# Modulation columns by one-column products, their later sums by 32 by 32 transposes, and a new order table

## The chip, the cores and the metric

The kernel runs on one core of a Trainium2 chip. The metric is the device time of one execution in microseconds (us). Five engines work side by side, each through its own list of instructions in a fixed order: TensorE (PE, with its weight loads as PEld), VectorE (DVE), ScalarE (ACT), GpSimd (POOL) and SyncE (SP), which issues nearly all of the DMAs. An instruction waits until its operands are there, and everything behind it on its engine waits with it.

## The reference, cut to what matters

One transformer block over 2048 rows of 576 numbers: a modulation vector from `c`, a linear attention with 32 heads of 18, and a feed-forward block with 4608 hidden units.

```python
mod = (_silu(c) @ w_mod).reshape(c.shape[0], 6, 1, -1)   # 576 -> 6 x 576
sa, ca, ga, sb, cb, gb = (mod[:, i] for i in range(6))
h = _layernorm(x) * (1 + ca) + sa
x = x + ga * _A_ref(h, A_wqkv, A_wo)      # linear attention: phi(q), phi(k), k^T v, divided by q . sum(k)
h = _layernorm(x) * (1 + cb) + sb
x = x + gb * _B_ref(h, B_w1, B_w2)        # silu(h @ w1) @ w2
```

The change touches how `mod` is summed. Its first third (`sa`, `ca`) is needed before any product with `h` can begin; the other two thirds (`ga`, `sb` and `cb`, `gb`) are needed much later.

## The kernel before, in words

Rows lie in 16 tiles of 128 (`x`, `acc`), the 576 columns in four chunks of 128 and a tail of 64. Numbers are split in a high and a low part, so that a product is three products of narrower numbers: for each chunk, high by high, low by high and high by low. Every operand therefore needs a high part (a cast, mostly by ACT, `w_hi`, `split_h`) and a low part (full minus high, by DVE or POOL, `w_lo`, `sub_hi`).

**The start.** `load_x`, `load_mod0` and `load_w` (lines 425 to 465) fetch row tiles, the first third of `w_mod` in four chunks of 128 rows (`mods`, in tiles called hT) with the last 64 rows apart (`tmod`), and the weights of K and Q (in tiles called acc). `load_mod0` fetches first the columns 0 to 256 of both halves, then the columns 256 to 576. Then:

- DVE multiplies each chunk of `w_mod` rows by silu(c), one number per partition (`sc`), and adds them up (`add_rows`, lines 517 and 519): four instructions for the first 256 columns and four for the other 320.
- TensorE sums over the 128 partitions. For the first two column chunks this is a product whose stationary operand is the summed tile and whose moving operand is a column of ones (`mod_cols`, line 528). For the rest the summed rows are the moving operand and the result is one row (`mod_rows`, line 539), which ACT and DVE copy out (`copy_row`, lines 543 and 544) and TensorE turns into columns (`turn_rows`, line 550).
- DVE adds 1 to the scale column (`add_cols`, line 533), applies shift and scale to the transposed rows (`modulate`, lines 360 and 362), and `split_h` makes high (line 366) and low part (line 262) of the result. `k_part` (line 574) multiplies them by the K weights for tiles 0 and 1. `keep_busy` (line 568) fills gaps on TensorE with products of ones that nobody reads.

**Stage A.** From there on K and Q of all tiles are projected (line 929), phi is applied (lines 936 to 942 and 495), k^T x is accumulated over blocks of four tiles (`sum_steps`: products in line 1054 in two PSUM rooms, psG0 and psG1, added to SBUF by DVE in line 1064), and the rows of the next block are normalised, turned and split (`block_steps`, `turn_steps`: lines 354, 1021, 362 and 998).

**The two later thirds of the modulation** (`mod_steps`) run beside stage A: SP loads chunks of `w_mod` into four rooms, ACT scales them (line 1102), POOL adds them up (line 1104, eight adds for each third), SP stores the sum of 128 partitions (590 KB) to DRAM (line 1105), ACT's queue loads it back so that the 128 partial sums of 9 columns lie side by side in a partition (line 1108), DVE sums them (line 1111), and SP stores the vector (line 1112).

**Attention's output and the MLP.** From 200 us to 360 us the output of attention, the second layer norm and the first group of hidden units run, in PSUM rooms called `big` (three of two banks) and `small` (two of one bank); `down_add` (line 1449) empties a `big`. From 360 us on come the other 17 groups, in PSUM rooms called `up` (line 1925) and `down` (line 2009) that take over the same eight banks.

**What sets the order.** The program is first written out by its loops and a planner; then `arrange(ORDERS, begun)` (called in line 2380, written in line 252) makes each engine follow a table of numbers, `ORDERS`: which of the instructions written out comes first, second and so on. The table covers everything up to some 460 us (2,991 of TensorE's products and 656 of DVE's instructions). Behind it the planner's own order stands. On SP the table also sets the order of the DMAs.

Of the kernel before, what the change touches and what calls it, by code (L numbers as in the profile page):

```python
# [24 lines left out]
def kernel(ctx: ExitStack, tc, A_x, A_wqkv, A_wo, B_x, B_w1, B_w2, c, w_mod, out):  # L25
# [33 lines left out]
    def behind(instructions):  # L59

        with ExitStack() as order:
# [7 lines left out]
            0-43 45-46 52 49-50 44 47-48 53-54 51 65 57-58 61-62 66-72 55-56 59-60 63-64 73-77 82-83 80-81 78-79  # L69
            116 84-87 90-91 124 88-89 92-105 117 106-111 125 118-123 112-115 126-141 154-173 142-147 174-177  # L70
            148-153 210-217 178-179 246-249 180-181 250-251 290-291 182-201 218-221 256-267 274-289 202-209
            292-295 302-319 222-227 320-329 228-237 268-273 330-331 296-299 332-335 300-301 336-337 238-245
            252-255 342-343 338-341 344-353 366-367 354-365 368-391 412-413 398-403 392-395 414-423 396-397
            406-411 424-425 436-439 426-427 440-445 404-405 446-451 428-435 452-457 462-463 458-461 464-517
            524-527 518-519 530-533 520-523 534-553 572-573 586-587 574-575 554-571 588-591 598-601 528-529
            592-595 602-609 596-597 610-629 576-579 630-645 580-585 646-653 658-661 682-685 662-669 686-687
            692-697 688-689 698-701 654-657 670-673 690-691 702-703 674-681 704-763 770-771 764-769 772-787
            826-829 788-825 838-843 862-865 830-833 844-845 866-867 846-857 872-875 834-837 890-891 876-877
            892-893 878-889 894-901 858-861 868-871 926-931 902-925 932-943 950-951 944-945 952-963 946-949
            978-983 1000-1001 966-977 984-999 1002-1015 1022-1027 1016-1021 1028-1029 964-965 1030-1075  # L80
            1084-1085 1076-1077 1102-1117 1086-1093 1130-1135 1118-1119 1078-1079 1120-1121 1136-1137 1122-1129
            1138-1139 1080-1083 1140-1145 1094-1095 1160-1161 1096-1101 1146-1157 1172-1177 1162-1171 1158-1159
            1248-1249 1178-1183 1250-1253 1184-1185 1254-1257 1186-1199 1208-1213 1258-1259 1285-1286 1200-1207
            1287-1292 1214-1219 1236-1237 1220-1227 1238-1247 1228-1235 1293-1300 1260-1284 1301-1339 1352-1356
            1340-1351 1357-1386 1413-1417 1387-1412 1418-1439 1446-1450 1440-1445 1451-1488 1507-1510 1489-1494
            1511-1513 1495-1506 1514-1558 1573-1576 1601-1604 1559-1572 1605 1577-1586 1634 1638 1587-1600
            1606-1623 1646-1649 1624-1625 1650 1655-1660 1626-1633 1661-1670 1639 1635-1637 1640-1641 1687-1688
            1671-1678 1715-1719 1679-1680 1642-1643 1681-1682 1651 1689-1694 1652-1653 1644-1645 1695-1698 1654
            1699-1710 1720-1727 1711-1712 1728-1731 1713-1714 1683 1748 1684-1685 1732-1745 1749 1686 1746-1747
            1776-1779 1781-1784 1780 1762 1785-1790 1763-1765 1791-1792 1750 1793-1798 1751-1761 1766-1771  # L90
            1799-1802 1772-1775 1854 1803-1809 1821-1825 1870 1810 1855-1857 1811 1826-1827 1812-1813 1871-1873
            1828-1831 1874-1876 1832-1835 1877 1836-1839 1814-1816 1858-1860 1883-1886 1817-1819 1861-1862 1820
            1840-1843 1863-1864 1844-1853 1865-1868 1915-1918 1869 1878-1882 1887-1904 1976 1990 1977-1980
            1919-1921 1905-1906 1922-1926 1991 1981 1907-1908 1931-1934 1982 1909-1914 1983-1984 1927-1930 1985
            1935 1992 1936-1941 1986 1942-1947 1987-1989 1948-1967 1993-1995 1968-1972 2004-2010 1973-1975
            2011-2022 1996-1999 2023-2028 2000 2029-2036 2001-2003 2037-2038 2049-2069 2039-2048 2070-2081 2086
            2082 2098-2099 2087-2088 2106-2110 2089-2095 2100-2101 2083-2085 2096-2097 2115-2136 2102 2137-2142
            2147 2159-2160 2103-2105 2111-2113 2161-2162 2148 2114 2187-2190 2163-2166 2149 2143-2146 2167-2168
            2150 2169-2186 2151 2191 2199 2192-2194 2200-2202 2152-2153 2203-2210 2195 2213 2211-2212 2154-2158
            2196-2198 2214-2224 2231-2234 2225-2230 2239 2249 2259-2261 2240 2235-2238 2262 2245 2241-2242  # L100
            2246-2247 2243 2255-2258 2248 2244 2265-2270 2295 2263 2250-2254 2271 2264 2272-2274 2296-2298
            2283-2284 2299-2305 2285-2287 2309 2288-2291 2277-2278 2292-2293 2310-2311 2275-2276 2312-2313 2294
            2306-2308 2279-2282 2314-2323 2329-2333 2335 2324 2336-2339 2334 2347-2352 2340 2353-2354 2325-2328
            2355-2358 2341 2359-2363 2342 2364-2365 2343-2344 2366-2369 2345-2346 2370-2375 2377 2376 2378-2382
            2391-2398 2383-2387 2399 2388-2389 2400-2402 2390 2403-2407 2427-2428 2408-2412 2421 2433 2413-2420
            2422 2445-2446 2434 2423-2426 2429-2432 2447-2450 2463-2470 2439 2435-2438 2440-2444 2483-2489
            2451-2452 2490 2457-2458 2503 2459-2460 2504 2461 2453 2462 2454-2456 2555-2560 2477-2480 2505-2508
            2521-2528 2471-2475 2481 2476 2482 2541-2544 2567-2569 2491-2493 2570-2572 2497-2502 2494-2496
            2545-2548 2515-2518 2509-2514 2519-2520 2579-2584 2529-2539 2585 2540 2593-2595 2549-2554 2561-2562
            2596 2563-2564 2597-2600 2586 2565-2566 2607-2610 2573-2574 2611-2612 2575-2577 2587-2589 2578  # L110
            2590-2592 2619-2623 2601 2624-2626 2633-2640 2613-2618 2647-2651 2602 2652 2603-2606 2641-2646
            2659-2663 2627-2630 2665-2667 2631-2632 2664 2668-2678 2653-2658 2693-2696 2685-2692 2739-2741
            2679-2683 2742-2743 2699-2704 2684 2711 2744 2697-2698 2712-2718 2705-2710 2725-2732 2719-2724
            2757-2761 2733-2738 2745-2756 2762 2775-2781 2795 2873-2874 2796-2798 2875-2876 2782 2877-2878
            2783-2786 2763-2774 2799-2800 2787-2794 2801-2804 2815-2820 2805-2814 2833-2840 2853-2855 2891 2856
            2892 2821 2841-2843 2822 2844 2823-2832 2857-2860 2845-2852 2861 2893 2929-2933 2879 2862 2880 2934
            2909-2911 2863-2864 2881-2890 2894-2895 2865-2866 2896 2867-2871 2897 2935 2898-2905 2872 2912-2916
# [483 lines left out]
    for k in range(HEAD):  # L601
        mod_cols(k, tmod, sel, first=k == 0)
    turn_tiles(pT, (0, 1), START)
    for k in (1, 2, 3):
        add_rows(k, 0, c1)
# [1806 lines left out]
```

## Time and profile before

| | us |
|---|---|
| median of three runs | 1092.07 |
| lowest and highest | 1091.23, 1094.24 |
| the profiled execution | 1092.31 |
| its span, first to last instruction | 1090.6 |

Times in the profile are counted from the first instruction. In a row of the timeline stand the start, the time that the instruction or the merged run of instructions (x4: four of them) took, the engine, the line of the kernel, the operation, and what is written and read. In brackets stands how long the engine had been idle, and what ended that. A row of stretches gives the busy time of each engine in a stretch of the span, the granted TensorE clock (PEclk, 1.00 is full) and what the DMA engines moved.

### The profile page before, as it was taken

What the parts mean: (1) busy time and instruction counts of PE and PEld (TensorE: products, weight loads), DVE (VectorE), ACT (ScalarE), POOL (GpSimd) and SP (SyncE); (2) the same over time, 40 slices, a digit from 0 to 9 for tenths busy, and PEclk for the clock granted to TensorE, in tenths of its full rate; (3) what the DMA queues carried; (4) which work ended last, traced back from release to release, by engine and by line L of the source; (5) the groups of instructions that cost most, each with busy time, mean ns of one, the idle gap of its engine ahead of it and who ended that gap; (6) DMA issues with size and microseconds to landing.
All of it is one profiled execution on the core that took longest, in us unless ns stands there. A gap on an engine that the chain in (4) does not pass through costs nothing.

```text
span 1090.6 us, 19057 instructions
## 1 busy us (share of the span) xinstructions
PE 1064.8 (98%) x7027; PEld 758.6 (70%) x7027; DVE 913.4 (84%) x1438; ACT 708.5 (65%) x1318; POOL 741.3 (68%) x804
## 2 busy tenths in 40 slices
PE   8899999999999899999999999999999999999998
PEld 6899999899785455666666666666666666666665
DVE  7968968778889799998997888987987887898767
ACT  5766554246757686677667767776776776676554
POOL 3556615655725499879878778877788678677563
PEclk9999999999999999999999999999999999999999
DMA  9497665223256768478577667567657747616522
GB/s 292 123 214 174 64 182 130 54 81 106 66 183 224 206 239 249 136 229 247 176 204 244 172 194 224 197 207 221 201 168 254 206 137 264 208 63 201 169 79 109
DMA packets 119342, 193.51 MB, mean 177 GB/s; under 512 B 42892, under 2 KB 77584, under 8 KB 119248
## 3 DMA queue, kind: packets, MB, share of 16 engines
q1 hardware_dynamic: 86276, 190.81, 56.2%
q10 hardware_dynamic: 32972, 1.48, 3.1%
q8 instruction: 55, 0.90, 0.3%
q14 instruction: 39, 0.32, 0.1%
HBM read 176.77 MB, written 15.48 MB: 176 GB/s over the span
## 4 chain that ended last, share of the span: by engine, by line
PE 77%; DVE 12%; ACT 3%; DMA 3%; issue 3%; POOL 2%; SPq 0%; DVEq 0%; POOLq 0%; ACTq 0%
PE up L1925 30%; PE down L2009 29%; PE big L390 6%; PE psK L929 4%; PE psG L1054 3%; DVE hT L262 1%; PE small L1433 1%; PE big L1444 1%; PE psK L1224 1%; DVE acc L1021 1%; DMA hT<-in_B_w_dram 1%; DMA turned<-acc 1%; PE big L1358 1%; DVE w L262 1%; DMA hT<-in_w_mod_dram 1%
## 5 line engine op out<-in xcount | busy, mean ns | idle before, releaser
L1925 PE MATMUL up<-hT,w 128*128 128x512 f16 x1264 | 317.6, 379 | 2.6 <-ACT p L1900 1.6
L1925 PEld LDWEIGHTS <-w 128*128 128x128 f16 x1492 | 146.0, 98 | 140.0 <-issue 3.9
L2018 DVE SCALAR_TENSOR_TENSOR acc<-acc,set,down 128x576 f32<-128x576 f32 x128 | 103.4, 810 | 31.4 <-PE down L2009 30.5
L1943 ACT ACTIVATE f<-f,set 128x512 f32<-128x512 f32 x102 | 73.0, 718 | 59.7 <-DVE f L1949 50.4
L1963 POOL TENSOR_TENSOR s<-f,f 128x256 f32<-128x256 f32 x66 | 55.2, 836 | 73.2 <-ACT f L1944 70.8
L2009 PE MATMUL down<-w,hc 128*128 128x288 f16 x600 | 90.8, 286 | 0.4 <-ACT f L1939 0.4
L2009 PE MATMUL down<-w,hb 128*128 128x288 f16 x600 | 90.5, 286 | 0.2 <-DVE acc L2018 0.2
L2009 PE MATMUL down<-w,hT 128*128 128x288 f16 x480 | 82.9, 286 | 0.4 <-DVE acc L2022 0.4
L1947 DVE TENSOR_TENSOR f<-up,p 128x512 f32<-128x512 f32 x102 | 69.6, 682 | 15.1 <-PE up L1925 8.6
L1944 ACT ACTIVATE f<-f,set 128x512 f32<-128x512 f32 x102 | 73.6, 722 | 3.2
L2009 PEld LDWEIGHTS <-hb 128*128 128x128 f16 x600 | 58.7, 98 | 22.6 <-issue 0.7
L2009 PEld LDWEIGHTS <-hc 128*128 128x128 f16 x600 | 58.6, 98 | 22.5 <-DVE acc L2018 0.7
L1949 DVE TENSOR_TENSOR f<-up,f 128x512 f32<-128x512 f32 x68 | 46.9, 689 | 26.6 <-PE up L1925 25.5
L1987 POOL TENSOR_TENSOR hc<-s,hc 128x512 f16<-128x512 f32 x50 | 63.7, 1274 | 6.4 <-ACT hc L1983 6.4
L1967 POOL TENSOR_TENSOR f<-f,s 128x256 f32<-128x256 f32 x66 | 53.6, 812 | 18.5 <-DVE hb L1987 10.2
L1960 POOL TENSOR_TENSOR s<-f 128x256 f32<-128x256 f32 x66 | 55.9, 847 | 14.1 <-ACT f L1940 11.3
L2009 PEld LDWEIGHTS <-hT 128*128 128x128 f16 x480 | 46.9, 98 | 26.6 <-issue 0.8
L390 PE MATMUL big<-w,qT 128*128 128x288 f32 x352 | 59.6, 307 | 0.6 <-DVE acc L1372 0.6
L1965 POOL TENSOR_TENSOR s<-s,f 128x256 f32<-128x256 f32 x66 | 56.4, 854 | 3.6
L2009 PE MATMUL down<-w,ha 128*128 128x288 f16 x396 | 55.6, 286 | 0.3 <-DVE w L262 0.3
L2009 PE MATMUL down<-w,hd 128*128 128x288 f16 x396 | 55.5, 286 | 0.2 <-ACT hd L1983 0.2
L1987 POOL TENSOR_TENSOR hd<-s,hd 128x256 f16<-128x256 f32 x66 | 50.5, 765 | 6.6 <-ACT hd L1983 6.6
(408 smaller groups left out, 2830.1 us busy)
## 6 DMA issues: line engine op xcount, KB each, us to landing
hT<-hd SPq DMA_DIRECT2D x101, 640.0 KB, 5.2
hT<-hd SPq DMA_DIRECT2D x65, 512.0 KB, 3.9
hT<-in_B_w_dram SPq DMA_DIRECT2D x14, 576.0 KB, 5.1
hT<-in_B_w_dram SPq DMA_DIRECT2D x28, 256.0 KB, 6.4
raw<-in_B_w_dram SPq DMA_DIRECT2D x11, 576.0 KB, 4.4
v<-in_B_w_dram SPq DMA_DIRECT2D x9, 576.0 KB, 5.1
acc<-in_A_x_dram SPq DMA_DIRECT2D x16, 288.0 KB, 5.0
raw<-in_B_w_dram SPq DMA_DIRECT2D x9, 512.0 KB, 5.6
```

Source lines behind the costliest of these rows:

```text
L390: T.matmul(ps, xpart(a), wpart(b), start=n == 0, stop=n == len(XW) - 1)
L1925: T.matmul(ps, left, right, start=first and m == 0, stop=m == len(seq) - 1, skip_group_check=True)
L1943: A.activation(f, f, AF.Silu, scale=factor(self.g, "inv"))
L1944: A.activation(f, f, AF.Identity, scale=factor(self.g, "delta"))
L1947: V.tensor_add(f, self.bank[bank[1]], self.p1)
L1960: G.tensor_sub(self.s3, half(i, 0, 0), half(i, 0, 1))
L1963: G.tensor_add(self.s[:, 0:1], half(i, 0, 1), half(i, 1, 1))
L1965: G.tensor_sub(self.s[:, 1:2], self.s[:, 0:1], half(i, 0, 0))
L1967: G.tensor_sub(half(i, 1, 0), half(i, 1, 0), self.s[:, 1:2])
L1987: eng.tensor_sub(t[:, :, 1, :], src, t[:, :, 0, :])
L2009: T.matmul(ps[:, p, :HALF], left[:, u, p * P : (p + 1) * P], right[:, v], start=n in (1, 5, 7, 6) and j == 0, stop=j == len(passes) - 1, s ...
L2018: V.scalar_tensor_tensor(dst, dst, factor(self.g, "ratio"), ps[:, :, :HALF], op0=ALU.mult, op1=ALU.add)
```

## The change

Three things change.

1. `add_rows`, `mod_rows`, `copy_row` and `turn_rows` go. For each chunk of 128 rows of `w_mod` and each 128 of its columns TensorE now makes a product with that 128 by 128 block as the stationary operand and silu(c) as a moving operand of one column (`mod_part`), all added up in PSUM: 16 products for the first two column chunks, 24 for the other three. POOL copies the 64 tail columns beside themselves (`twice`), since the tail's columns are wanted in both halves of the partitions. Fourteen of the 33 `keep_busy` products go.
2. `mod_steps` no longer stores and loads the 590 KB. DVE transposes the sum in blocks of 32 by 32 (two instructions), sums each row of a block (a sum over 32 numbers), SP stores the 18 KB that are left and loads them with the four partition groups side by side, DVE sums those four, and SP stores the vector as before, in another order of elements.
3. Every number of `ORDERS` is new; the comment on the change says that the table comes from a model in which VectorE and GpSimd exclude each other. In the code that is written out, the last part of the K weights is loaded ahead of row tiles 2 and 3. The work outside 1 and 2 is the same, instruction for instruction.

```diff
     ORDERS = {
         "PE": """
-            0-43 45-46 52 49-50 44 47-48 53-54 51 65 57-58 61-62 66-72 55-56 59-60 63-64 73-77 82-83 80-81 78-79
+            0-29 38-42 45-49 30-33 50 34-37 43-44 51-56 65-70 79-90 57 59-60 63-64 73-74 139 58 61-62 71-72
...
-    colps = kvp[0][:, 1, 128:], kvp[2][:, 1, :]
+    colps = psT(), kvp[0][:, 1, 128:]
     colp = {k: colps[k >= HEAD][:, 2 * k : 2 * k + 2] for k in START}
...
+    def twice(m):
+        G.tensor_copy(m[..., D:DX], m[..., KC * P : D])
+
+    def mod_tail(js):
+        for j in js:
+            T.matmul(colp[j], tmod[:, j * P : (j + 1) * P], sel, start=j == js[0], stop=False, skip_group_check=True)
+
+    def mod_part(k, js):
+        for j in js:
             for a in range(2):
-                T.matmul(colp[k][:, a : a + 1], m[:, a, k * P : (k + 1) * P], rhs,
-                         start=first and a == 0, stop=last, skip_group_check=True)
+                T.matmul(colp[j][:, a : a + 1], mods[k][:, a, j * P : (j + 1) * P], sc[:, k : k + 1],
+                         start=False, stop=k == KC - 1, skip_group_check=True)
...
     w_hi(wk_, 1, acc[1])
-    for a in range(2):
-        mod_rows(a, 0)
-    first_k(1)
+    w_lo(wk_, 1, acc[1], V)
+    twice(tmod)
+    mod_tail(range(HEAD, KC + 1))
+    for k in range(KC):
+        twice(mods[k])
+        mod_part(k, range(HEAD, KC + 1))
+        if k < HEAD:
+            first_k(k)
+    add_cols(HEAD, KC + 1)
...
-        do("SP", 0.45, lambda: nc.sync.dma_start(parts, tmod2[:, :, 0:D]), ["tmod0", "tmod1"], [f"parts{piece}"], 8.0)
...
-        do("SP", 0.45, lambda: nc.scalar.dma_start(r, parts.rearrange("p a d -> p (a d)").rearrange("p (q j) -> q p j", j=NC9)),
-           [f"parts{piece}"], raws2[i], 14.0)
-        s9 = s9s[piece - 1]
-        do("DVE", 2.27, lambda: V.tensor_reduce(s9, r.rearrange("q p j -> q j p"), axis=AX.X, op=ALU.add), raws2[i], [f"s9{piece}"])
...
+        def turn():
+            for a in range(2):
+                V.transpose(r[:, a].rearrange("p (b i) -> p b i", i=32), tmod2[:, a, 0:D].rearrange("p (b i) -> p b i", i=32))
+
+        def fold():
+            V.tensor_reduce(some, flat.rearrange("p (b i) -> p b i", i=32), axis=AX.X, op=ALU.add)
+            nc.sync.dma_start(quarters, some)
+            nc.sync.dma_start(four, quarters.rearrange("(q c) b -> c q b", q=4))
+            V.tensor_reduce(total, four.rearrange("c q b -> c b q"), axis=AX.X, op=ALU.add)
```

Three places of the order are shown, each as it stood and as it stands. The first is the list of SP at the very start: xt are row tiles, hT the first third of `w_mod` (256 columns of both halves, then 320), acc0, acc1 and acc2 the weights of K and Q (the first five pieces are K's), acc3 with 128x4x576 the four row tiles of the next block. Before:

```order
L427 DMA xt_118<-in_A_x_dram 128x576 x2
L451 DMA hT_125<-in_w_mod_dram 128x2x256 x4
L394 DMA acc0_91<-in_A_wqkv_dram 128x576 x2
L451 DMA hT_125<-in_w_mod_dram 128x2x320 x4
L394 DMA acc0_91<-in_A_wqkv_dram 128x576 x2
L427 DMA xt_118<-in_A_x_dram 128x576 x2
L394 DMA acc1_92<-in_A_wqkv_dram 128x576
L396 DMA acc1_92<-in_A_wqkv_dram 64x576
L1005 DMA acc3_94<-in_A_x_dram 128x4x576
L397 DMA acc1_92<-in_A_wqkv_dram 64x576
```

And now:

```order
L426 DMA xt_118<-in_A_x_dram 128x576 x2
L450 DMA hT_125<-in_w_mod_dram 128x2x256 x2
L426 DMA xt_118<-in_A_x_dram 128x576
L450 DMA hT_125<-in_w_mod_dram 128x2x256
L426 DMA xt_118<-in_A_x_dram 128x576
L450 DMA hT_125<-in_w_mod_dram 128x2x256
L450 DMA hT_125<-in_w_mod_dram 128x2x320 x4
L393 DMA acc0_91<-in_A_wqkv_dram 128x576 x2
L959 DMA acc3_94<-in_A_x_dram 128x4x576
L393 DMA acc0_91<-in_A_wqkv_dram 128x576 x2
L395 DMA acc1_92<-in_A_wqkv_dram 64x576
L396 DMA acc1_92<-in_A_wqkv_dram 64x576
```

The first K weights moved from behind the first 256 modulation columns to behind all row tiles and all modulation columns, and the third K weight to behind the next block's rows as well.

The second place is DVE in stage A, from the first of block 1's sums to the third (sum0, sum1, sum2, read from psG0 and psG1). Before:

```order
L1064 TENSOR_TENSOR sum0_107<-psG1_117,sum0_107 128x576
L1064 TENSOR_TENSOR sum1_108<-psG0_116,sum1_108 128x576
L942 TENSOR_SCALAR acc1_92<-psK_220 128x576
L495 SCALAR_TENSOR_TENSOR acc1_92<-e_98,acc1_92 128x576
L362 TENSOR_SCALAR acc2_93<-acc2_93,col_a_84 128x512 x2
L1064 TENSOR_TENSOR sum2_109<-psG1_117,sum2_109 128x576
```

And now:

```order
L1018 TENSOR_TENSOR sum0_107<-psG1_117,sum0_107 128x576
L1018 TENSOR_TENSOR sum1_108<-psG0_116,sum1_108 128x576
L896 TENSOR_SCALAR acc1_92<-psK_233 128x576
L1067 STREAM_TRANSPOSE raw1_122<-tmod_381 128x576 x2
L1070 TENSOR_REDUCE crow_96<-raw1_122 128x36
L1018 TENSOR_TENSOR sum2_109<-psG1_117,sum2_109 128x576
```

The two transposes and the first sum of the last third of the modulation (tmod is what POOL's adds made) now stand ahead of sum2; the second step of phi and the two modulations of turned rows moved behind it.

The third place is DVE around the end of the first group of hidden units, where the PSUM rooms `big` give way to `up`. In the built program the first room `up` lies in the bank of big_3881 before, and in the bank of big_3935 now. Before:

```order
L1449 SCALAR_TENSOR_TENSOR acc3_94<-acc3_94,set0_99,big_3923 128x576
L268 SCALAR_TENSOR_TENSOR w_3657<-raw_3660,set0_99,w_3657 128x256
L1449 SCALAR_TENSOR_TENSOR acc3_94<-acc3_94,set0_99,big_3881 128x576
L268 SCALAR_TENSOR_TENSOR w_3657<-v_3658,set0_99,w_3657 128x256 x2
L268 SCALAR_TENSOR_TENSOR w_3657<-raw_3660,set0_99,w_3657 128x256
L1947 TENSOR_TENSOR f01_4005<-up_3997,p1_3995 128x512
```

And now:

```order
L1415 SCALAR_TENSOR_TENSOR acc3_94<-acc3_94,set0_99,big_3893 128x576
L261 TENSOR_TENSOR S_3684<-S_3682,S_3684 128x512
L1415 SCALAR_TENSOR_TENSOR acc3_94<-acc3_94,set0_99,big_3907 128x576
L267 SCALAR_TENSOR_TENSOR w_3669<-raw_3672,set0_99,w_3669 128x256
L1415 SCALAR_TENSOR_TENSOR acc3_94<-acc3_94,set0_99,big_3935 128x576
L261 TENSOR_TENSOR S_3820<-H_3464,S_3820 128x512
```

On TensorE the products of big_3881 and big_3923 were mixed to the end, so that both were emptied only then; now the last eleven products all go to big_3935, and the other rooms are finished earlier.

More of the change, by code (lines that the diff above doesn't have):

```diff
@@ L596 @@
     pT = rooms(ps2()[:, 0, :])
-    rows = [psT()[0:1], kvp[0][0:1].rearrange("p a b -> p (a b)")]
-    row = [e_[0:1], zsum[0:1]]
     keep_busy(11)
-    for k in range(HEAD):
-        mod_cols(k, tmod, sel, first=k == 0)
+    mod_tail(range(HEAD))
+    for k in range(KC):
+        mod_part(k, range(HEAD))
     turn_tiles(pT, (0, 1), START)
-    for k in (1, 2, 3):
-        add_rows(k, 0, c1)
+    add_cols(0, HEAD)
     kps = [ps2() for _ in range(2)]
@@ L886 @@
     xT = accb[NB - 2].rearrange("p a d -> p (a d)")
-    NC9 = 2 * D // P
-    s9s = [crowp[:, 64 + 16 * i : 64 + 16 * i + NC9] for i in range(2)]
+    NB32 = 2 * D // 32
     turned = [dram.tile([D, 4, P], F32, name=f"turned{b}") for b in range(1, NB)]
-    parts_of = [dram.tile([P, 2, D], F32, name=f"parts{i}") for i in (1, 2)]
+    quarters_of = [dram.tile([P, NB32], F32, name=f"quarters{i}") for i in (1, 2)]
     vec_of = [dram.tile([2, D], F32, name=f"vec{i}") for i in (1, 2)]
```

294 lines of the change are left out of this document (126 added, 168 removed).

## The prediction

> **What bounds the kernel now.** I read the page first, then the stretches, then what TensorE waited for, then the timeline at the longest waits.
>
> ```profile
> span 1090.6 us, 19057 instructions
> ...
> PE 1064.8 (98%) x7027; PEld 758.6 (70%) x7027; DVE 913.4 (84%) x1438; ACT 708.5 (65%) x1318; POOL 741.3 (68%) x804
> ```
>
> TensorE is the bound: 25.8 us of the span are not busy. The stretches, cut where the stages change, tell where they lie (start and end, length, then busy time of PE, PEld, DVE, ACT, POOL).
>
> ```profile
> 0.00:31.10 31.10, 26.56 (x170) 21.83 (x171) 24.02 (x61) 17.73 (x33) 10.45 (x14) 1.00 0.91 287
> 31.10:200.00 168.90, 160.98 (x1204) 158.60 (x1202) 133.84 (x191) 95.66 (x148) 90.75 (x65) 1.00 0.64 138
> 200.00:360.00 160.00, 154.87 (x1090) 131.94 (x1091) 137.34 (x252) 95.41 (x156) 82.14 (x76) 1.00 0.41 130
> 360.00:470.00 110.00, 106.17 (x616) 59.76 (x615) 101.76 (x154) 79.36 (x163) 89.50 (x109) 0.98 0.64 200
> 470.00:1073.00 603.00, 602.94 (x3850) 376.44 (x3849) 504.87 (x762) 414.56 (x812) 462.92 (x538) 1.00 0.62 193
> ```
>
> From 470 to 1073 us TensorE rests for 0.06 us, and the table of orders ends at some 460 us: there is nothing to win there and nothing is moved. What the change can win is TensorE's idle time up to 470 us: 4.5 + 7.9 + 5.1 + 3.8 = 21.3 us, besides fillers and products that run slowly. The largest single waits of TensorE (total, times, longest):
>
> ```profile
> PE up L1925 <- ACT S L1632: 2.1, 1, 2.1
> PE psG L1054 <- DVE sum L1064: 1.8, 2, 1.3
> ...
> PE psK L929 <- DVE hT L998: 1.6, 1, 1.6
> ...
> PE psK L929 <- DVE hT L262: 1.3, 1, 1.3
> ```
>
> They are short and many; no single cause holds the time. So I cost the start, the entry into `up`, and the waits behind DVE, and leave the rest alone.
>
> **The start.** What goes from DVE: six sums of 814 ns, two first multiplications, and a copy of a row. What comes to TensorE has a price from line 528, whose products have the same shape: four in 0.51 us, so 0.13 each at most, and 40 x 0.13 = 5.2 us. What goes there: 14 fillers and eight products with one row (line 539, two in 0.70 us: 2.8 us), the eight of line 528 (1.0) and the fillers at about the same 0.13 (1.8): 5.6 us. On TensorE that is even.
>
> ```profile
> L519 DVE SCALAR_TENSOR_TENSOR hT<-hT,sc 128x512 f32<-128x512 f32 (+1 forms) x6 | 4.9, 814 | 0.1
> ...
> 12.30 0.51 PE L528 MATMUL psG<-ones,hT 128*128 128x1 f32 x4
> 15.53 0.70 PE L539 MATMUL psG<-tmod,sc 64*1 64x320 f32 x2
> 14.80:31.10 16.30, 15.13 (x95) 11.50 (x96) 15.99 (x35) 10.30 (x20) 7.64 (x6) 1.00 0.95 299
> 16.96 0.67 ACT L471 CAST w<-acc 128x576 fp32r<-128x576 f32 x1 [1.56 <-DMA acc<-in_A_wqkv_dram]
> 25.64 0.67 ACT L471 CAST v<-acc 128x576 fp32r<-128x576 f32 x1
> 31.09 1.10 PE L929 MATMUL psK<-wq,hT 128*128 128x288 f32 x7
> ```
>
> Between the first K product (14.80) and the first Q product (31.09) DVE is busy for 15.99 of 16.30 us: there DVE is the bound, not TensorE, and DMA moves 299 GB/s. Now the order of the loads, in MB (a tile or a weight chunk is 128 x 576 x 4 bytes = 0.295, the first third of `w_mod` 2.36 + 0.295). Before, ahead of the end of the third K weight stood 0.59 + 0.295 + 2.36 + 0.885 = 4.13, and ACT waited for it until 16.96. Now the same 4.13 = 1.18 + 0.295 + 2.36 + 0.295 stand ahead of the end of the first K weight: it lands at about 16.9, its cast (0.67) ends at 17.6, and the first K product comes 2.8 us later than today. By then all modulation columns are there. The last K weight lands behind 2.36 MB more (one K weight, the next block's four tiles, three K weights), at 16.96 + 2.36 / 0.299 = 24.9, about 0.8 us before its cast starts today (25.64). From there today's chain needs 31.09 - 25.64 = 5.45 us, so the first Q product comes at 30.3. By DVE it is 17.6 + 16.3 less three of the sums (2.4), 31.5; but DVE rests for 31.1 - 24.02 = 7.1 us in the whole start, and the new order moves statistics and modulations ahead of the first K product. I allow 3 us for them (an estimate, under half of that rest): 28.5. I take 29.5, between these: **-1.6 us**. Ends: -2.6 (28.5), and +2.8 if the whole stretch only shifts. GpSimd's five copies of 64 columns are hidden as long as POOL stays half idle (busy for 7.64 of those 16.3 us with six instructions, 1.27 each); without that cover five such instructions cost at most 6.4 us.
>
> **The entry into `up`.** Here is the dearest wait.
>
> ```profile
> 352.31 5.32 PE L1444 MATMUL big<-w,hs 128*128 128x288 f16 x42 [0.18 <-DVE acc L1449]
> 357.66 0.81 DVE L1449 SCALAR_TENSOR_TENSOR acc<-acc,set,big 128x576 f32<-128x576 f32 x1 [0.31 <-PE big L1444]
> 358.39 0.48 DVE L268 SCALAR_TENSOR_TENSOR w<-raw,set,w 128x256 f16<-128x256 f32 x1
> 358.79 0.81 DVE L1449 SCALAR_TENSOR_TENSOR acc<-acc,set,big 128x576 f32<-128x576 f32 x1
> 359.70 4.44 PE L1925 MATMUL up<-first,w 128*128 128x512 f16 x12 [2.08 <-ACT S L1632]
> 360.00:362.00 2.00, 2.00 (x6) 0.68 (x5) 0.79 (x2) 0.00 (x0) 1.39 (x2) 0.50 0.36 82
> 363.97 1.46 PE L1925 MATMUL up<-hT,w 128*128 128x512 f16 x6
> ```
>
> The profile names ACT, but ACT's cast was over before; the first `up` takes the bank of big_3881, whose emptying ends at 358.79 + 0.81 = 359.60, behind big_3923 and a split on DVE. That is 2.08 us of nothing. Then the granted clock is 0.50, and twelve products take 4.44 us instead of the 2 x 1.46 = 2.9 that the later row gives: 1.5 us more. In the new order only one room is emptied after the last product, so the gap is one emptying of 0.81 and about 0.1: 0.9 us, a gain of 1.1. Gaps of 1.3 to 1.6 us elsewhere (the waits above) stand in stretches at clock 1.00, so I take the clock to stay: **-2.6 us**. Ends: -1.1 with the clock falling all the same, 0 if DVE comes late with its splits. The Trainium skill, in "TensorE: Matmul & The Clock Gate", Part 1, says that the clock halves after an idle window of about 3.4 us; a gap of 2.08 us was enough here, so the measurement decides. Taken literally, that page would leave the slow products to something else, and the sum below would be 1.5 us higher.
>
> **The waits behind DVE.** Some DVE instructions take many times their usual time while POOL works.
>
> ```profile
> L678 DVE TENSOR_TENSOR xs<-xt,xs 128x64 fp32r<-128x64 f32 x2 | 0.4, 222 | 0.1
> 41.61 1.49 POOL L963 TENSOR_TENSOR w<-a,w 128x576 fp32r<-128x576 f32 x1
> 41.73 1.46 DVE L980 TENSOR_TENSOR xs<-xt,xs 128x64 fp32r<-128x64 f32 x1
> ...
> 43.11 1.64 DVE L262 TENSOR_TENSOR hT<-raw,hT 128x256 fp32r<-128x256 f32 x1
> ...
> 97.70 1.44 POOL L1104 TENSOR_TENSOR tmod<-tmod,raw 128x576 f32<-128x576 f32 x1 [4.87 <-ACT raw L1102]
> 102.12 3.39 POOL L1104 TENSOR_TENSOR tmod<-tmod,acc 128x576 f32<-128x576 f32 x2
> 102.58 3.21 DVE L362 TENSOR_SCALAR acc<-acc,col_a 128x512 f32<-128x512 f32 x2
> ...
> 105.47 1.59 POOL L966 TENSOR_TENSOR zsum<-zsum,a 128x576 f32<-128x576 f32 x1
> 105.71 0.74 DVE L1064 TENSOR_TENSOR sum<-psG,sum 128x576 f32<-128x576 f32 x1
> ```
>
> A 64-column subtraction takes 0.22 us in the start and 1.46 beside POOL; it ends as POOL's instruction ends (43.1), and the next one, of 256 columns, takes 1.64. So POOL and DVE shut each other out, and a model that knows it plans truer. TensorE's waits for hT (1.3), for L998 (1.6) and for sum2 (1.3, at 106.5, behind two L362 that took 3.21) come from it: 4.2 us. A new order can remove them and make others. I take half: **-2.0 us**, ends -4.2 and, as a rival, a loss. But the sum that reads PSUM took 0.74 us beside POOL's 1.59. The Trainium skill, "SBUF — State Buffer", Who interferes with whom, says the same and speaks against a blanket rule: only a DVE instruction with two SBUF inputs or in a two-port mode contends with GpSimd. If the model excludes every pair, it plans around collisions that don't exist; this term would then be 0 and the time 1088.1.
>
> **The later sums.** Removed for each third: a store and a load of 590 KB and a sum of 2392 ns; added: two transposes of 748, a sum over the same 1152 numbers, at most 2392, a small one, and two small DMAs. On DVE that is +0.7 to +1.9 us each, off TensorE's path while DVE is idle 35 of 169 us in that stretch: 0. If that cover is gone, up to +3.8.
>
> ```profile
> L1111 DVE TENSOR_REDUCE crow<-raw 128x9 f32<-128x1152 f32 x2 | 4.8, 2392 | 0.0
> L1021 DVE STREAM_TRANSPOSE acc<-xt 128x576 f32<-128x576 f32 x12 | 8.4, 748 | 0.3
> 99.72 0.76 DVE L1064 TENSOR_TENSOR sum<-psG,sum 128x576 f32<-128x576 f32 x1 [1.10 <-PE psG L1054]
> 113.32 0.56 SPq L1105 DMA_DIRECT2D parts<-tmod  x1
> ```
>
> **Sum.** The profiled execution took 1092.3 us, 0.2 above the median: 1092.3 - 1.6 - 2.6 - 2.0 = 1086.1. I predict 1086.
>
> **Rivals.** *Slower: DVE waits for POOL's adds.* In the second place shown, the transposes need all eight adds of the last third. Today those run from 97.70 to 113.3 (the store of their sum). DVE comes to the transposes right behind sum1, at about 101. sum2, the splits and the emptying of K and Q rooms queue behind them. If the adds end as late as today, sum2 ends at 113.3 + 1.5 + 2.4 + 0.8 = 118.0 instead of 106.45: 11.5 us, of which TensorE pays all but the 1.3 that it waits today, so 1092.3 - 1.6 - 2.6 + 10.2 = 1098.3. It decides from adds that end after about 110, where the loss exceeds the other terms by 3.3 us. For it: POOL's last rooms are loaded through the same SP list, which now also waits for DVE's first sums. Against it: without the 590 KB round trip the rooms come free earlier, and POOL rests for 4.87 us just before 97.70. Chance 0.18. *Same: the waits only move.* The start shifts by +2.8, the entry gains its 2.6, the DVE waits return elsewhere: 1092.5. For it: DVE is busy for 137 of 160 and 102 of 110 us from 200 to 470, so a wait that is moved meets other work there. Chance 0.20. *Faster by more:* all three DVE waits go and the start gains its most: 1092.3 - 2.6 - 2.6 - 4.2 = 1082.9. Chance 0.15.
>
> **Numbers.** The forecast, between 1083.5 and 1088.8, has 0.47. About 0.3% (3.3 us) is what a measurement of this kernel can tell from no change. Faster: 0.47 + 0.15 = 0.62, same 0.20, slower 0.18. The range goes from 1078 (the faster case and a few waits more) to 1097 (into the slower case).
>
> **What would show it.** Right: the first Q product near 29.5 us, a gap of about 0.9 us ahead of the first `up` and clock 1.00 behind it, no wait above 1 us for sum2 or for the split of turned rows, and 470 us to the end as long as now. Wrong: a DVE gap ahead of the first transposes of tmod in the last third and TensorE waiting for sum2 right after; a first Q product after 31; half clock near 360 us; or new waits of more than 1 us between 110 and 350 us that add up to the gain.

## The result, and the profile after

The changed kernel takes 1106.35 us (1106.04 to 1107.66), the kernel before 1093.15 us beside it: ratio 1.0118, 95% interval 1.0085 to 1.0150. It is slower by 13 us where 6 us less were forecast, and lies outside the stated range. The profiled execution took 1106.04 us, its span is 1104.3 us. Below, a single execution of the run with 16 columns is left out of the comparison: it took 1842.87 us at a mean granted clock of 0.556, and what held the clock down there is unknown.

The stretches are cut at TensorE's milestones: first Q product, first product that reads the sums of stage A, first `up`, first `down` of turned rows, end (columns as in the prediction, and behind them the granted clock, the busy share of the DMA engines and GB/s). First the changed kernel, then the kernel before.

```profile
0.00:39.95 39.95, 38.51 (x206) 37.56 (x206) 17.82 (x56) 19.23 (x36) 10.57 (x19) 0.74 0.66 215
39.95:204.90 164.95, 158.06 (x1154) 155.00 (x1154) 116.39 (x177) 91.64 (x142) 84.10 (x60) 0.99 0.47 129
204.90:372.05 167.15, 158.86 (x1140) 137.19 (x1139) 144.71 (x264) 95.94 (x157) 83.52 (x84) 1.00 0.38 122
372.05:494.17 122.12, 115.66 (x681) 66.12 (x681) 106.24 (x170) 88.16 (x180) 94.34 (x117) 1.00 0.66 209
494.17:1104.30 610.13, 605.72 (x3889) 380.31 (x3887) 506.60 (x769) 412.71 (x803) 460.60 (x532) 1.00 0.60 189
```

```profile
0.00:31.09 31.09, 26.55 (x169) 21.82 (x170) 24.01 (x61) 17.72 (x33) 10.45 (x14) 1.00 0.91 287
31.09:193.27 162.18, 155.52 (x1154) 153.47 (x1153) 128.37 (x180) 95.02 (x147) 85.97 (x61) 1.00 0.67 143
193.27:359.70 166.43, 160.04 (x1141) 136.90 (x1139) 142.52 (x262) 96.06 (x157) 86.92 (x80) 1.00 0.39 125
359.70:480.46 120.76, 116.93 (x681) 66.27 (x681) 112.13 (x169) 87.64 (x180) 97.30 (x119) 0.99 0.65 206
480.46:1090.60 610.14, 605.72 (x3889) 380.17 (x3887) 506.39 (x770) 412.01 (x803) 460.69 (x532) 1.00 0.61 190
```

The start is 8.86 us longer, the second stretch (called the Q stretch below) 2.77, the way to `up` 0.72, the first groups 1.36; the rest is equal to 0.01 us. In the start TensorE is busy for 38.5 of 39.95 us, at a mean granted clock of 0.74, and VectorE for 17.8: the bound has changed sides. The timeline of TensorE in the changed kernel's start (start, duration, line, shape, count of records), and two windows of the start:

```profile
10.45 1.93 PE L519 MATMUL psG<-sc,hT 128*128 128x1 f32 x16
...
18.01 10.24 PE L519 MATMUL psG<-sc,hT 128*128 128x1 f32 x48
28.11 2.03 PE L546 MATMUL psK<-w,hT 128*128 128x288 f32 x7
...
39.95 1.33 PE L883 MATMUL psK<-wq,hT 128*128 128x288 f32 x8
```

```profile
10.00:13.00 3.00, 3.00 (x30) 3.00 (x29) 0.89 (x3) 1.93 (x4) 0.00 (x0) 1.00 1.08 366
13.00:34.00 21.00, 21.00 (x102) 20.97 (x100) 11.11 (x31) 8.61 (x17) 6.07 (x8) 0.51 0.62 214
```

Two things stand there. The 40 one-column products leave 80 records (instructions in the trace), not 40. And from 13 to 34 us the clock is half, although TensorE has no idle time at all in those 21 us: 48 records take 10.24 us (0.213 each), where the first 16 take 1.93 (0.112 from one to the next).

Behind the start, TensorE's largest waits in the changed kernel (total, times, longest):

```profile
PE psG L1008 <- ACT w L913: 3.1, 3, 2.0
PE down L1975 <- DVE acc L1984: 3.0, 2, 2.4
PE big L1410 <- DVE hs L267: 3.0, 2, 2.7
PE up L1891 <- DVE acc L1415: 2.0, 1, 2.0
```

The waits for hT and sum2 that the prediction quoted are gone; others of the same size stand in their place. At the entry into `up`:

```profile
370.07 0.81 DVE L1415 SCALAR_TENSOR_TENSOR acc<-acc,set,big 128x576 f32<-128x576 f32 x1
370.79 0.48 DVE L267 SCALAR_TENSOR_TENSOR w<-raw,set,w 128x256 f16<-128x256 f32 x1
371.19 0.81 DVE L1415 SCALAR_TENSOR_TENSOR acc<-acc,set,big 128x576 f32<-128x576 f32 x1
372.05 1.67 PE L1891 MATMUL up<-first,w 128*128 128x512 f16 x7 [2.01 <-DVE acc L1415]
```

Two emptyings and a split still stand between the last product and the first `up`, so the wait is 2.01 us as before; but the clock stays at 1.00 behind it.

### The profile page after: what moved, and what is told of

It reads as the page before. It is cut to its first block, busy times and chain, and to the rows that moved or that the text cites. A ratio compares the mean times of both kernels' runs of the same rounds, so it can differ in the third digit from the quotient of the medians.

```text
span 1104.3 us, 19123 instructions
## 1 busy us (share of the span) xinstructions
PE 1076.8 (98%) x7063; PEld 776.2 (70%) x7063; DVE 891.8 (81%) x1432; ACT 707.7 (64%) x1316; POOL 733.1 (66%) x809
## 4 chain that ended last, share of the span: by engine, by line
PE 85%; DVE 10%; issue 2%; ACT 1%; DMA 1%; POOL 1%; SPq 0%; ACTq 0%; DVEq 0%; POOLq 0%
PE up L1891 31%; PE down L1975 29%; PE big L389 7%; PE psK L883 5%; PE psG L1008 4%; PE psG L519 1%; PE big L1410 1%; DMA raw<-in_w_mod_dram 1%; PE small L1399 1%; PE psK L1190 1%; PE psG L540 1%; PE big L1324 1%; DVE w L267 1%; DVE w L261 1%; DVE hT L261 1%
## 5 line engine op out<-in xcount | busy, mean ns | idle before, releaser
L1008 PE MATMUL psG<-w,xs 128*128 128x288 f32 x336 | 53.9, 299 | 2.9 <-DVE w L915 1.2
```

The lines of the kernel that those rows point to most:

```text
L1008: T.matmul(ps[:, h, :HALF], l, pk[t][:, u, h * HALF : (h + 1) * HALF], start=t == 0 and m == 0, stop=t == 3 and m == len(left) - 1)
```

## The experiments

**One-column products by themselves, and fillers among them.** A kernel of its own streams 60 one-column products, then the same with a filler (a 128 x 128 product) behind every fourth, second, single one, then 60 products of 32 and of 64 columns, with fillers before each stretch.

> A kernel by itself, with none of the reference's work: 128 x 128 products of ones to warm TensorE, then six stretches with such warm products between them: 60 one-column products alone; one filler (a 128 x 128 product) behind every fourth, every second, every one-column product; 60 products of 32 columns; 60 of 64 columns. TensorE never waits for data. Theory A (TensorE's clock is granted by how much of the time it streams columns, and one-column products only load weights): the clock falls to 0.50 within about 4 us of the first stretch, start to start goes from 0.111 us to 0.213 us a record, and it comes back in the filler streak behind. Where a share of fillers suffices the stretch stays at 0.111 us. Rival B (the clock fell in the changed kernel for another reason: idle gaps, the phase of the start): all stretches stay at 1.00 and 0.111 us a record.

Its windows (start and end, length, busy time of PE, PEld, DVE, POOL, granted clock, DMA): one column from 29.6 us on, then the later part of each stretch, in the order above:

```profile
29.50:32.00 2.50, 2.50 (x25) 2.50 (x23) 0.00 (x0) 0.00 (x0) 0.97 0.00 0
32.00:53.00 21.00, 21.00 (x100) 21.00 (x100) 0.00 (x0) 0.00 (x0) 0.50 0.00 1
...
80.00:102.50 22.50, 22.50 (x106) 22.50 (x107) 0.00 (x0) 0.00 (x0) 0.50 0.00 1
...
131.00:150.00 19.00, 19.00 (x91) 19.00 (x91) 0.00 (x0) 0.00 (x0) 0.50 0.00 1
172.40:188.40 16.00, 16.00 (x146) 16.00 (x145) 0.00 (x0) 0.00 (x0) 1.00 0.00 1
...
212.80:230.00 17.20, 17.20 (x83) 17.20 (x83) 0.00 (x0) 0.00 (x0) 0.50 0.00 1
251.80:265.20 13.40, 13.40 (x123) 13.40 (x122) 0.00 (x0) 0.00 (x0) 1.00 0.01 1
```

TensorE is busy throughout, and the clock falls about 2.3 us after the one-column products begin. One filler to four products or to two doesn't hold it, one to one does; 32 columns don't, 64 do. At full clock a record takes the same 0.111 us from 1 to 64 columns wide, and 0.112 with 128, so the measure that fits is the mean number of columns in a record: 32 and (1 + 1 + 128) / 3 = 43 fall, 64 and (1 + 128) / 2 = 64.5 hold. Theory A stands, in one execution of this kernel: of the two, it is the columns that stream and not the busy time that the clock follows.

**Fillers in the changed kernel.** Behind every second product:

```diff
+                if next(one_col) % 2 == 1:
+                    filler_behind(m, 1)
```

> The changed kernel with one 128 x 128 filler product behind every second one-column product (20 fillers, 40 records), nothing else moved. Theory A: the clock stays at 1.00 from about 13 to 34 us; 140 records of 0.111 us instead of 100 at up to 0.213, first K product at about 25.6 us (28.1 before), first Q product at about 35 (39.95), time 1106.35 - 5 = 1101. If one in three isn't enough to hold the clock: 40 x 0.213 = 8.5 us later instead, 1115. Rival B (the loss is the order: all one-column products ahead of the first K product, and the clock costs nothing): 40 more products on a TensorE that is busy, 4.4 to 8.5 us slower, 1111 to 1115.

```profile
13.00:34.00 21.00, 21.00 (x101) 21.00 (x100) 4.94 (x14) 5.72 (x10) 4.65 (x7) 0.50 0.62 207
```

1112.19 us, ratio 1.0172 (1.0137 to 1.0208) to the kernel before: one to two doesn't hold the clock here either. The 40 records more cost less than the 8.5 us that were expected: the first Q product comes at 46.00, 6.05 later. This run alone couldn't tell A from B; with the stretch of the kernel by itself it agrees with A.

**The kernel before without its fillers.** Its 14 fillers after the first 11 us are left out:

```diff
         for _ in range(n):
+            if n < 8:
+                ...
+                continue
             T.matmul(...)
```

> The kernel before without its 14 fillers after the first 11 us (7 products at 11.4, 12.7 and 13.5 us, 7 from 19.9 to 24.9); the other 19 at the start stay. Theory A1 (the clock fell because the change took these fillers out): the clock is 0.50 over most of 14 to 30 us, first Q product at 36 or later, time +4 to +9 us. Theory A2 (it fell because of the one-column products, of which this kernel has only eight records): clock 1.00, first Q product at 31 +- 0.5, time the same within 1 us.

```profile
13.00:31.10 18.10, 17.00 (x56) 11.31 (x57) 13.83 (x34) 8.19 (x17) 6.51 (x7) 0.50 0.83 268
```

Here too the clock is 0.50 in the start, which A2 excluded: the old start holds its clock only by its fillers. The first Q product comes at 35.21 instead of 31.09, and the time is 1096.11 us, ratio 1.0032 (1.0018 to 1.0046), both a little less than A1 gave (36 or later, 4 us or more). So the change took away what held the clock and added products that let it fall; the next pair shows that the second can be mended by itself.

**The same products, wider.** Each product streams 64 columns: its own column of silu(c), and zeros that add nothing to its neighbours' columns.

```diff
+    behind_it(one, V.memset(zsum[:, : W * (KC + 1) - 1], 0.0))
+    behind_it(exp, A.copy(zsum[:, W - 1 : W * KC : W], sc[:, 0:KC]))
...
-                T.matmul(colp[j][:, a : a + 1], mods[k][:, a, j * P : (j + 1) * P], sc[:, k : k + 1], ...)
+                s0 = W - 1 + W * k - 2 * j - a
+                T.matmul(colps[j >= HEAD][:, :W], mods[k][:, a, j * P : (j + 1) * P], zsum[:, s0 : s0 + W], ...)
```

> The changed kernel, same 40 products with the same weights in the same order, but each streams 64 columns instead of one: the column of silu(c) it needs, and zeros that add nothing to the other columns (added: one memset on VectorE, one copy of four columns on ScalarE). In the kernel by itself a 64-column record took the same 0.111 us as a one-column one and the clock stayed at 1.00. Theory A (the clock follows the share of time in which columns stream): clock 1.00 from 13 to 34 us, 48 records behind 18 us take 5.3 us instead of 10.2, first K product near 23.5 (28.1), first Q product near 33 (39.95), time -7: 1099. Rival B (the loss is the order or the number of these products): no change, 1106 +- 2.

```profile
14.17 5.62 PE L527 MATMUL psG<-zsum,hT 128*128 128x64 f32 x48
20.20 1.20 PE L554 MATMUL psK<-w,hT 128*128 128x288 f32 x7 [0.40 <-ACT w L471]
...
30.02 1.19 PE L893 MATMUL psK<-wq,hT 128*128 128x288 f32 x7
```

```profile
13.00:34.00 21.00, 19.69 (x146) 18.01 (x146) 17.33 (x42) 15.67 (x31) 10.39 (x11) 1.00 0.72 241
```

The clock is 1.00, the 48 records take 5.62 us instead of 10.24, and the first Q product comes at 30.02 us, 9.9 earlier (theory A gave 33). Time 1099.22 us, ratio to the kernel before 1.0067 (1.0042 to 1.0091).

The control, W = 16:

> The control of the run with 64 columns: the same instructions, 16 columns wide. In the kernel by itself 32 columns let the clock fall. Theory A: the clock is 0.50 from about 13 us on as in the changed kernel, first Q product at 37 to 40, time 1106 +- 2. If the 64-column run is faster for another reason (the zeroed buffer, the copy, another bank), this one is as fast as that.

1107.83 us, ratio 1.0129 (1.0108 to 1.0151), clock 0.53 from 11 to 33 us, first Q product at 39.17. The same instructions with too few columns gain nothing: A is shown, B has fallen.

**The waits from 104 to 110 us.** In the changed kernel ACT, VectorE and GpSimd read:

```profile
101.03 1.26 ACT L1056 ACTIVATE raw<-raw,sc 128x1152 f32<-128x1152 f32 x1 [5.03 <-DMA raw<-in_w_mod_dram]
104.06 1.72 DVE L915 SCALAR_TENSOR_TENSOR w<-a,w 128x576 fp32r<-128x576 f32 x1 [4.96 <-ACT w L913]
105.12 7.18 POOL L1058 TENSOR_TENSOR tmod<-tmod,acc 128x576 f32<-128x576 f32 x4
```

One number of ACT's table is moved, so that the scaling no longer stands ahead of the K features:

```diff
- ... 89 94 101 96-98 102 100 99 ...
+ ... 89 94 96-98 102 100-101 99 ...
```

> The changed kernel with one number moved in ACT's order: the scaling of the fourth chunk of the second third of w_mod (line 1056, which stood waiting 5.0 us for its load at 101 us) goes behind the six ACT instructions of the K features that stood behind it. Theory C (TensorE's waits from 104 to 110 us, 5 us, and the half clock behind them, come from the features waiting in ACT's queue behind that load): these waits fall below 1.5 us in sum, time -4 to -6 us (1100.5 to 1102.5). Rival D (they come from VectorE's instructions being stretched by GpSimd's adds, 1.7 and 2.0 us instead of 0.75): the waits stay at 3 us or more, time within 2 us of 1106.

```profile
109.67 0.76 DVE L877 TENSOR_SCALAR acc<-psK 128x576 f32<-128x576 f32 x1 [3.78 <-POOL tmod L1039]
112.56 0.78 DVE L1048 STREAM_TRANSPOSE raw<-tmod 128x576 f32<-128x576 f32 x1 [2.13 <-POOL crow L1098]
...
116.84 3.49 PE L989 MATMUL psG<-w,xs 128*128 128x288 f32 x13 [4.36 <-DVE sum L999]
```

The waits at 104 to 110 are gone, as C says, but TensorE waits 4.36 us for the block sum at 116.84 instead, because VectorE's transposes, ahead of that sum, wait for GpSimd's last adds (from 112.53). The time is 1107.69 us, no gain. That is the place and the mechanism of the slower rival, at less than half its price of 10.2 us. Then the transposes too are moved, behind the sum and four more instructions (the expectation counts ten):

```diff
- ... 137 129 128 183 134 138 135 139 144 145 ...
+ ... 137 134 138 135 139 144 129 128 183 145 ...
```

> The changed kernel with two moves in its orders: the scaling on ACT as in the run before, and on DVE the two transposes of the second later third and their sum (lines 1067 and 1070) go behind the third block sum and ten instructions more, to where GpSimd's adds are over. Theory C2 (the stretch of the Q products lost its time because VectorE, in order, waits for GpSimd's adds to tmod, which the new order puts ahead of the block sum): the wait of 4.4 us at 117 us in the run with ACT's move alone is gone, no wait of TensorE above 2 us from 100 to 125 us, the stretch from the first to the last Q product is 4 to 6 us shorter than 165, time 1101 to 1103. Rival D2 (something behind it is late too, the load or the turned rows): the wait moves on, time 1105 to 1107.

```profile
111.64 0.82 ACT L314 ACTIVATE acc<-acc,col_a 128x512 f32<-128x512 f32 x1 [7.15 <-DMA acc<-turned]
...
125.18 3.73 PE L838 MATMUL psK<-w,hT 128*128 128x288 f32 x14 [3.95 <-DVE hT L907]
```

The wait moves on once more, to the turned rows of the next block: 1107.5 us. ACT awaits the load of the first of them until 111.64, and VectorE's splits of these rows (line 907) come at 113.14, where one takes 2.83 us while GpSimd adds, and then only at 123.85, behind the transposes that were moved. How much of the 3.95 us each of these makes isn't shown. C2 has fallen as an explanation of lost time: taking one wait away uncovered another, twice.

**All of it together**, with 64 columns, both moves, and at the entry the four emptyings ahead of the splits:

```diff
- 482 497 488 496 487 498 478 499
+ 482 497 496 498 499 488 487 478
```

> The changed kernel with the 64-column products, the moves on ACT and DVE, and at the entry into up the last four emptyings (line 1415) ahead of the three splits that stood between them on DVE. If the terms add up: -7 (start), -4.5 (adds), -1.1 (the entry's wait falls from 2.0 to 0.9 us): 1093.5, which is level with the kernel before (1092.9). If they hide one another, 1096 to 1100.

```profile
361.60 1.67 PE L1856 MATMUL up<-first,w 128*128 128x512 f16 x7 [1.01 <-DVE acc L1380]
```

The entry's wait is 1.01 us, near the 0.9 of the prediction. But 1098.42 us (1096.14 to 1106.56, ratio 1.0066, 1.0037 to 1.0096) is within the spread of the 64-column kernel alone (1097.12 to 1104.75): only the start's share is plain. In this profile too the clock is 1.00 in the start, yet the first Q product comes at 31.39.

**The old order behind the new start.** Up to the first Q product each engine keeps the new order; behind it the same instructions stand in the sequence of the kernel before.

> The 64-column kernel, whose start (up to the first Q product) keeps the changed kernel's order, but behind it every engine follows the order table of the kernel before: the same instructions, put into the old sequence; the new transposes and folds of the later sums stand where GpSimd's adds of that third were over in the old order. Theory F (behind the start the new order is dearer than the old one: by the profiles 2.3 us in the Q stretch, 1.5 to the entry of up, 2.4 from there to the first down of turned rows): first Q product at 30, the three stretches at 162, 166.5 and 119 to 121, time 1099.2 - 6 = 1093, level with the kernel before. Rival G (the loss behind the start lies in the changed code, the later sums by transposes, whatever the order): 1098 to 1100.

1094.09 us over 12 executions (1091.97 to 1101.10), ratio 1.0027 (1.0009 to 1.0046): by the ratios 4.4 us less than with the new order, though the two intervals overlap. The profiled execution is one of the long ones, 1101.01 us, and shows why:

```profile
11.00:32.00 21.00, 21.00 (x101) 20.60 (x100) 9.27 (x27) 10.26 (x19) 5.24 (x8) 0.51 0.74 246
```

With 64 columns the clock fell in this execution; the two shortest, 1091.97 and 1092.03 us, have a mean clock of 1.000. The entry's emptying ahead of a split:

```diff
- 472 499 473 496
+ 472 499 496 473
```

> As after_wide64_old, and the emptying for which the first up product waits goes ahead of the split of weights in front of it on DVE. The wait at the entry into up falls from 2.1 to about 1.6 us; if the clock then stays up (it fell behind 2.08 us in the kernel before, and didn't fall behind 2.01 us in the changed one), 0.5 to 2 us less than the run before: 1091 to 1092.5, otherwise no change that can be measured.

1094.25 us (1091.39 to 1104.20): no change that can be measured. The wait falls to 1.68 us, and in this profile too the clock is 0.51 from 11 to 32 us.

**The kernel before once more.**

> The kernel before once more, for a second profile. If its clock in the start and at the entry into up is a matter of the order alone, the same rows come again: 0.50 from 360 to 363 us, 1.00 elsewhere. If it hangs on where the monitoring falls in time, other stretches at 0.50 show up, and the stretches differ by 1 to 4 us.

```profile
26.00:30.00 4.00, 3.83 (x17) 3.82 (x18) 3.76 (x10) 3.93 (x8) 0.00 (x0) 0.58 0.51 158
...
362.18 2.75 PE L1925 MATMUL up<-first,w 128*128 128x512 f16 x12 [2.07 <-ACT S L1632]
```

1093.44 us. This time the half clock lies at 26 to 30 us, and none is at the entry into `up`: behind the same wait the twelve products take 2.75 us, not 4.44. So the slow products at 360 us, from which the prediction took 1.5 us, come in some executions and not in others. The new order doesn't settle it either: behind its wait of 2.0 us the clock is 1.00 in the changed kernel's profile, but 0.59 from 372.70 to 375.70 us in that of the run with both moves. The Trainium skill, in "TensorE: Matmul & The Clock Gate", Part 1, says that the window over which activity is judged runs free of the kernel, so that the same kernel changes clock at other points from run to run; these two profiles agree with that.

**A pair with the clock held in the start**, 112 columns wide, new order and old order:

> As after_wide64 (new order throughout), with products of 112 columns. A 128-column record takes 0.112 us at full clock, as a one-column one does, so the wider stream should cost nothing. If 64 columns sit near the bound of what holds the clock (it held in one profile of such a kernel and fell from 11 to 32 us in another), 112 columns hold it in more executions: mean clock 0.992 or more in every execution, none above 1101 us, median 1097 to 1099. If the share of streaming isn't what decides, the spread stays as with 64 columns (1097 to 1105).

> As after_wide64_old (old order behind the start), with 112 columns. Theory F (behind the start the new order is dearer) in a pair whose starts are alike: 4 to 6 us less than after_wide112, median 1092 to 1094, and at equal mean clock 3 us less or more. Rival G (the code of the later sums, or the clock alone, makes the difference): within 2 us of after_wide112.

The new order takes 1098.40 us (1096.26 to 1100.33, ratio 1.0054, 1.0033 to 1.0075), the old order 1094.20 us (1091.85 to 1095.89, ratio 1.0017, 1.0003 to 1.0031). With 112 columns no execution of either is above 1100.4. The old order takes 4.2 us less by medians, as theory F said, but its second condition isn't met: the mean clock is 0.992 to 0.997 with the new order and 0.997 to 1.000 with the old one, and at the one value that both have, 0.997, a single execution of the new order (1096.26 us) stands against seven of the old one with a median of 1094.62, a difference of 1.6 us. So a part of the 4.2 us may come through a lower clock. In the profile of the new order that is a clock of 0.53 from 100 to 105 us, right behind the waits on ACT and VectorE in the Q stretch (0.77, 1.21 and 1.97 us); in that of the old order the clock is 1.00 there. A part that the clock doesn't make is seen in the stretch from the first `up` to the first `down` of turned rows, which has a clock of 1.00 in both. New order, then old, and what TensorE waited for most there:

```profile
362.04:484.15 122.11, 115.65 (x681) 66.02 (x681) 105.99 (x170) 88.00 (x180) 94.38 (x117) 1.00 0.66 208
...
PE down L1985 <- DVE acc L1994: 3.0, 2, 2.4
```

```profile
361.95:480.64 118.69, 115.20 (x681) 65.91 (x682) 111.73 (x169) 87.66 (x180) 97.35 (x119) 1.00 0.66 210
...
PE up L1787 <- ACT S L1494: 2.1, 1, 2.1
```

3.4 of the 3.7 us by which the spans of these two executions differ (1094.5 and 1090.8) lie there; TensorE is idle for 6.46 us of it with the new order and for 3.49 with the old. The Q stretch is as long in both (164.94 against 165.15), although the new order runs a part of it at half clock. In the changed kernel itself that wait is at 457 us:

```profile
454.82 0.64 DVE L695 TENSOR_SCALAR set<-set 128x4 f32<-128x4 f32 x1
455.49 0.58 DVE L697 TENSOR_TENSOR set<-set 128x1 f32<-128x1 f32 x1
456.11 0.65 DVE L702 TENSOR_TENSOR set<-set,fixed 128x1 f32<-128x1 f32 x1
456.68 1.53 DVE L1984 SCALAR_TENSOR_TENSOR acc<-acc,set,down 128x576 f32<-128x576 f32 x2
457.54 0.40 PE L1975 MATMUL down<-w,ha 128*128 128x288 f16 x2 [2.40 <-DVE acc L1984]
```

Three one- and four-column instructions of the factors, 0.6 us each beside GpSimd (lines 697 and 702 take 0.15 and 0.16 us at 373.1 us), stand on VectorE ahead of the emptying that `down` needs.

## Why the prediction was wrong, step by step

- **The step that failed** is the price of the start on TensorE: "four in 0.51 us, so 0.13 each at most, and 40 x 0.13 = 5.2 us", with the fillers that go counted at their own price, "On TensorE that is even". First a count: a row's x4 counts records, and a product of this kind leaves two; 80 x 0.111 = 8.9 us even at full clock. The 14 fillers leave 28 records too, 3.1 us and not 1.8, so 6.9 us go and 8.9 come. Second, what mattered: the fillers were priced as time saved, not as what holds the clock. Without them, and with 80 records that stream one column, the clock is half from 13 to 34 us in the profile, and the mean clock is 0.985 to 0.989 in all four executions of the changed kernel. The 80 records cost 15.9 us, and the K products behind them begin at 28.11 us, not 17.6. Worth, by the ratios to the kernel before: 1.0118 with one column, 1.0054 with 112, so 0.0064 x 1092 = 7.0 us, with 2 to 4 us of uncertainty in each ratio; the spans of the two profiled executions differ by 9.8 us (1104.3 and 1094.5).
- **The rest of the start came out near its figure, in part by luck.** With the clock held the first Q product comes at 30.02, 30.25, 30.49 and 31.39 us in four profiles, where the working gave 29.5 (28.5 to 33.9). But its two halves were both off, and against each other. The first K product was to come at 17.6, right behind the landing of its weights and with all modulation columns there. With 64 columns wide it comes at 20.20, when ACT is done with a cast of those weights that it only reaches at 18.90, behind its other work; the second set of columns is finished by VectorE at 20.64. From there to the first Q product it takes 9.8 us, where the working had 11.9. VectorE's relief is there (busy for 18.06 us of that start, 24.01 before), but a bound that goes from VectorE to TensorE needed TensorE's clock.
- **The entry into `up`, -2.6.** The wait was to fall to 0.9 us and stayed at 2.01: the order puts an older emptying and a split ahead of the one that counts. I had looked at which bank the first `up` takes, not at how far VectorE is behind when its products end. The slow products, the other 1.5 us, come and go between executions of one kernel.
- **The waits behind VectorE, -2.0.** The waits quoted are gone, but the idle time of TensorE in the Q stretch is 6.89 us (6.66 before), and a wait of 2.4 us at 457 us is new. With equal starts the new order costs 4.2 us by medians, a part of it perhaps through the clock. The rival "the waits only move" was the better reading here. That the model's exclusion of VectorE and GpSimd is the cause isn't shown: I compared the two orders, not two models.
- **The slower rival** (VectorE's transposes wait for GpSimd's adds) is real, as the run with ACT's move shows, but it is not what cost the time: in the changed kernel VectorE doesn't wait ahead of the transposes (115.06 us), and where it did, taking the wait away gained nothing.
- **From 470 us on nothing moves**: right, 610.13 against 610.14 us.

What stays open: 1094.20 against 1091.88 us, the kernel before in the same comparison. With the old order and the clock held the start is 0.6 us shorter (30.49 against 31.09) and the Q stretch 3.0 longer (165.15 against 162.18). Whether the code of the later sums or the seam between the two orders costs that wasn't tried. Nor was the changed kernel with one column and all its fillers, so how the loss in the start divides between the fillers that went and the narrow products that came isn't known. No version here beats the kernel before.

## What to carry to other kernels

Before a product that keeps TensorE warm is taken out, or a wide product is replaced by a narrow one, count the columns that stream, not the busy time: narrow products whose records take as long as wide ones (here 0.111 us from 1 to 112 columns) may be made wider for nothing, and that can hold the clock. Count records and instructions apart before a price is multiplied. And when an order is changed as a whole, test it as a whole against the old one behind an equal start; a single wait that it removes says nothing about the next one in the queue.

## What the runs showed of the hardware

- TensorE's clock fell to 0.50 with no idle time at all: about 2.3 us after one-column products of f32 began, 4.1 us after those of 32 columns. 64 columns held it in the one execution of the kernel by itself but not in every execution of the whole kernel. With 112 columns none of 18 executions had a mean clock below 0.992; a half clock from 11 to 32 us, as in the profile with 64, is worth 0.010 of it. The Trainium skill, in "TensorE: Matmul & The Clock Gate", Part 1, says that the clock is set by how busy TensorE has been recently; here it fell while TensorE was busy for all of the time, so by these runs records with few columns don't count as records with many do.
- The spread between executions goes with the clock: of the 17 of the kernel before beside the last pair, the five at a mean clock of 1.000 took 1089.66 to 1090.76 us, the five at 0.995 took 1092.41 to 1093.47.
